# Value features in six chunks of six whole heads (120 rows) instead of five chunks of 128 rows

## The chip, the cores and the metric

The kernel runs on one core of one Trainium2 chip. The metric is device microseconds of one execution, start to end. Each run also has a *span*, the time from the first to the last instruction that the profiler recorded; the time is somewhat longer than the span. Each profile shows one execution. Wherever a median is quoted, it is over all runs of that kernel in that set of rounds.

TensorE (PE) multiplies matrices, and loads its weights (PEld) in parallel; VectorE is DVE, ScalarE is ACT, GpSimd is POOL, and SP issues the DMAs. A *pass* here is one matmul instruction.

## The reference, cut to what matters

```python
xn = _layernorm(x)                                  # x: 1 x 2048 x 640, H = 32 heads, Dh = 20
q, k, v = split(xn @ wqkv)                          # each 32 heads of 20 features
pq, pk = phi(q), phi(k)
kv  = einsum("bhsd,bhse->bhde", pk, v)              # one 20 x 20 matrix per head
num = einsum("bhqd,bhde->bhqe", pq, kv)
den = einsum("bhqd,bhd->bhq", pq, sum of pk over s)
s   = (num / den) @ wo                              # 640 x 640
g   = silu(relu(xn @ w1) @ w2)                      # 640 -> 1728 -> 640
out = x + s * g
```

Attention is linear and its `kv` is block diagonal (32 blocks of 20 x 20). The kernel forms G = xn^T pk, from it the blocks kv = wv^T G, and *folds* the output projection in: W = kv wo, 640 x 640. Then s is one product of the divided pq with W.

## The kernel before: the parts that matter

The 640 value features are cut into C = 5 chunks of P = 128 rows. A boundary of 128 cuts a head of 20, so a chunk touches 7 or 8 heads, and neighbouring chunks share heads.

```python
h_lo = [(P * c) // DH for c in range(C)]
h_hi = [-(-(P * (c + 1)) // DH) for c in range(C)]
def cs_of_m(m):       # chunks whose heads reach into columns 128m .. 128m+127 of W's rows
    return [c for c in range(C) if DH * h_lo[c] < P * (m + 1) and DH * h_hi[c] > P * m]
# -> 2, 3, 3, 3, 2 chunks for m = 0..4: 13, times two halves of 320 columns: 26 passes

def kv_block(c, b):                                  # one PSUM bank b
    n0, n1 = DH * h_lo[c], DH * h_hi[c]              # 140 or 160 columns
    PE:  for k in range(C): matmul(ps[b][:, 0:n1-n0], lhsT=wv_sb[:, k, P*c:P*(c+1)], rhs=GT[:, k, n0:n1])
    DVE: kvp[:, c, n0:n1] = ps[b][:, 0:n1-n0] * mask # also waits for POOL's memset of kvp

def W_block(m):                                      # banks b and b+1; pairs (4,5) and (6,7) in turn
    PE:  for a in range(2):
           for c in cs_of_m(m): matmul(ps[b+a][:, 0:320], lhsT=kvp[:, c, P*m:P*(m+1)], rhs=wo_sb[:, c, 320*a:320*(a+1)])
         # ONE signal, after the last pass of both halves
    ACT: wf[:, m, 0:320]   = ps[b]
    DVE: wf[:, m, 320:640] = ps[b+1]
# ... (cut)
# SP queue, in order: w2 (2 DMAs), w2l (2), wo (1), rx (5: reciprocals of the denominator, read back), ...
# PE order: G, half of U(0), kv_block 0..4, half of U(0), half of U(1), W_block 0..4, half of U(1), ...
# DVE order: divide(0), divide(1) [need rx 0 and 1], the masks of kv_block, divide(2..4), ...
```

`U(p)` are the passes of the second feed-forward product; U(1) holds banks 0 to 3 open while W is made, so W has two bank pairs and no more.

## Time and profile before

| what | value | where it is read |
|---|---|---|
| time | 226.27 us (226.14 to 226.59) | runs |
| span of the profiled run | 224.6 us | page |
| PE busy | 218.1 us, 97% | page, part 1 |
| PE's share of the chain that ended last | 92% | page, part 4 |
| kv blocks | 25 passes, 1.56 us | chain of waits |
| W blocks | 26 passes, 3.55 us | chain of waits |

The page of the kernel before, parts 1 and 4: busy time and share by engine, then the chain of work that ended last.

```profile
span 224.6 us, 3494 instructions
...
PE 218.1 (97%) x1450; PEld 135.2 (60%) x1460; DVE 102.5 (46%) x191; ACT 88.3 (39%) x146; POOL 43.8 (20%) x62
...
PE 92%; DVE 2%; DMA 2%; issue 1%; ACT 1%; SPq 1%; POOL 0%; DVEq 0%
```

TensorE is the bottleneck nearly everywhere, so a stage is worth what TensorE spends in it. The same chain in order of time, before (start, duration in us, what): L714 is kv, L729 is W, L768 is U.

```profile
137.66 1.56 PE psT L714 x25
139.23 3.53 PE psT L768 x26
...
143.47 3.71 PE psT L768 x26
147.18 3.55 PE psT L729 x26
```

The timeline of before in the W stage (start, duration, engine, line, operation, count, and in brackets how long the engine was idle before and what ended it): L735 and L733 are the copies that empty a block.

```profile
147.02 3.71 PE L729 MATMUL psT<-reg 128*128 128x320 bf16 x26
...
147.76 0.49 DVE L735 CAST reg<-psT 128x320 bf16<-128x320 f32 x1 [4.79 <-PE psT L729]
147.82 0.43 ACT L733 ACTIVATE reg<-psT 128x320 bf16<-128x320 f32 x1
148.36 2.03 PEld L729 LDWEIGHTS psT<-reg 128*128 128x128 bf16 x16 [0.16 <-DVE reg L735]
```

TensorE runs the 26 passes as one piece. Its only wait is for the first DVE copy: the weight load is 0.16 us late, and since weights are loaded ahead, the passes themselves lose 0.02 us.

### The profile page before, as it was taken

How to read it: one execution, taken by the hardware profiler on the slowest of the kernel's cores; microseconds unless marked ns; L12 is line 12 of the kernel's file. 1: busy time of each engine (PE TensorE's matmuls, PEld its weight loads, DVE VectorE, ACT ScalarE, POOL GpSimd, SP SyncE). 2: the span in 40 equal slices, each digit the busy share in tenths (PEclk: the TensorE clock that was granted, in tenths of full speed). 3: DMA queues.
4: the chain of work that ended last, by engine and by line, in shares of the span. 5: the costliest groups of instructions: out<-in, count | busy, mean ns of one | idle time of the engine just before them, and what ended most of it. 6: DMA issues, size and time to landing. Idle time of an engine off the chain costs nothing.

```text
span 224.6 us, 3494 instructions
## 1 busy us (share of the span) xinstructions
PE 218.1 (97%) x1450; PEld 135.2 (60%) x1460; DVE 102.5 (46%) x191; ACT 88.3 (39%) x146; POOL 43.8 (20%) x62
## 2 busy tenths in 40 slices
PE   7999999999999999999999999999999999999993
PEld 7654555455554555444477778667767767776772
DVE  4599931796639872967000044440404041331445
ACT  4587765657665666654521122241021102102110
POOL 2436842322541255700000013000000000000000
PEclk9999999999999999999999999999999999999999
DMA  6999620012501150000999999500001010101021
GB/s 185 362 395 257 149 74 0 0 31 58 32 1 29 29 56 5 0 0 3 210 217 300 346 386 325 176 0 3 34 25 61 0 60 3 58 0 61 27 90 58
DMA packets 24239, 23.07 MB, mean 103 GB/s; under 512 B 8992, under 2 KB 23584, under 8 KB 24224
## 3 DMA queue, kind: packets, MB, share of 16 engines
q1 hardware_dynamic: 24224, 22.86, 35.7%
q8 instruction: 11, 0.18, 0.4%
q14 instruction: 4, 0.03, 0.1%
HBM read 15.65 MB, written 5.24 MB: 93 GB/s over the span
## 4 chain that ended last, share of the span: by engine, by line
PE 92%; DVE 2%; DMA 2%; issue 1%; ACT 1%; SPq 1%; POOL 0%; DVEq 0%
PE psT L768 25%; PE psT L514 25%; PE psT L702 10%; PE psT L491 10%; PE psT L439 9%; PE psT L796 8%; DMA reg<-in_A_x_dram 2%; PE psT L729 2%; PE psT L746 1%; PE psT L527 1%; DVE reg L810 1%; PE psT L714 1%; PE psT L610 1%; DVE reg L813 0%; DVE stats L383 0%
## 5 line engine op out<-in xcount | busy, mean ns | idle before, releaser
L768 PE MATMUL psT<-reg,hT 128*128 128x320 bf16 x416 | 58.7, 299 | 0.3
L514 PE MATMUL psT<-reg 128*128 128x512 bf16 x252 | 56.8, 379 | 0.5 <-issue 0.2
L768 PEld LDWEIGHTS psT<-reg,hT 128*128 128x128 bf16 x416 | 40.3, 98 | 17.0 <-PE psT L746 1.6
L514 PEld LDWEIGHTS psT<-reg 128*128 128x128 bf16 x260 | 25.2, 98 | 29.2 <-ACT hT L518 0.4
L764 ACT ACTIVATE reg<-psT 128x640 bf16<-128x640 f32 x16 | 10.8, 702 | 68.8 <-PE psT L746 35.4
L518 ACT ACTIVATE hT<-psT 128x512 bf16<-128x512 f32 x52 | 30.9, 599 | 17.7 <-PE psT L514 17.4
L810 DVE TENSOR_TENSOR reg<-psT,reg 128x640 bf16<-128x640 f32 (+1 forms) x18 | 13.5, 749 | 49.0 <-PE psT L796 45.9
L451 POOL TENSOR_TENSOR zacc<-zacc,reg 128x640 f32<-128x640 f32 x16 | 22.6, 1412 | 21.5 <-DVE reg L470 21.3
L439 PE MATMUL psT<-reg 128*128 128x320 bf16 x160 | 24.5, 299 | 0.1
L796 PE MATMUL psT<-reg,pqT 128*128 128x320 bf16 x160 | 22.9, 299 | 0.0
L702 PE MATMUL psT<-reg 128*128 128x320 bf16 x160 | 21.9, 299 | 0.0
L491 PE MATMUL psT<-reg 128*128 128x512 bf16 x98 | 21.8, 379 | 0.1
L439 PEld LDWEIGHTS psT<-reg 128*128 128x128 bf16 x160 | 15.4, 98 | 8.0 <-ACT reg L427 0.3
L702 PEld LDWEIGHTS psT<-reg 128*128 128x128 bf16 x160 | 15.6, 98 | 6.4 <-issue 0.4
L796 PEld LDWEIGHTS psT<-reg,pqT 128*128 128x128 bf16 x160 | 15.7, 98 | 6.1
L695 DVE TENSOR_TENSOR pqT<-pqT,reg 128x2048 bf16<-128x2048 bf16 x5 | 5.9, 1219 | 26.8 <-DMA reg<-rden_by_feature 26.8
L491 PEld LDWEIGHTS psT<-reg 128*128 128x128 bf16 x100 | 9.8, 98 | 11.2
L383 DVE BATCH_NORM_STATS2 stats<-reg 128x6 f32<-128x320 bf16 x32 | 14.1, 479 | 3.7 <-DMA reg<-in_A_x_dram 3.7
L498 ACT ACTIVATE er<-psT 128x512 bf16<-128x512 f32 x20 | 12.4, 619 | 8.6 <-PE psT L491 3.5
L456 ACT ACTIVATE ek<-psT 128x640 bf16<-128x640 f32 x16 | 11.3, 707 | 9.1 <-PE psT L439 9.1
L468 DVE TENSOR_SCALAR ek<-ek 128x640 bf16<-128x640 bf16 x16 | 5.5, 347 | 18.3 <-ACT ek L456 18.3
L508 DVE SCALAR_TENSOR_TENSOR pqT<-er 128x512 bf16<-128x512 bf16 x15 | 12.9, 859 | 0.5
(58 smaller groups left out, 139.2 us busy)
## 6 DMA issues: line engine op xcount, KB each, us to landing
reg<-in_A_x_dram SPq DMA_DIRECT2D x16, 160.0 KB, 5.3
rden_by_feature<-rden SPq DMA_DIRECT2D x4, 640.0 KB, 8.8
reg<-rden_by_feature SPq DMA_DIRECT2D x5, 512.0 KB, 11.1
reg<-in_A_x_dram SPq DMA_DIRECT2D x4, 640.0 KB, 6.8
reg<-in_B_w_dram SPq DMA_DIRECT2D x2, 1120.0 KB, 10.2
out_dram<-reg SPq DMA_DIRECT2D x14, 160.0 KB, 1.8
reg<-in_B_w_dram SPq DMA_DIRECT2D x1, 1040.0 KB, 10.2
reg<-in_B_w_dram SPq DMA_DIRECT2D x1, 960.0 KB, 14.8
```

The lines of the kernel that those rows point to most:

```text
L383: sc.op("DVE", lambda eng: eng.bn_stats(stats[:, t, a, :], xin[:, t % XR, HN * a:HN * (a + 1)]), R=[("xin", t % XR)], W=[("stats", t, a)])
L439: fns.append(lambda eng, a=a, k=k: eng.matmul(ps[b + a][:, 0:HN], lhsT=xnT[:, k, tok(t)], rhs=wqk[:, k, D + HN * a:D + HN * (a + 1)], star ...
L451: sc.op("POOL", lambda eng: eng.tensor_tensor(out=zacc[:, :], in0=zacc[:, :], in1=pk[:, t, :], op=ALU.add), R=[("zacc",), ("pk", t)], W=[( ...
L491: sc.group("PE", [(lambda eng, k=k: eng.matmul(ps[b], lhsT=wqk[:, k, P * f:P * (f + 1)], rhs=xnT[:, k, schunk(j)], start=(k == 0), stop=(k ...
L498: sc.op("ACT", lambda eng: eng.activation(out=e_, in_=ps[b], func=ACTF.Exp), R=[("ps", b)], W=[("er_e", es)])
L508: sc.op("DVE", lambda eng: eng.scalar_tensor_tensor(out=pqT[:, f, schunk(j)], in0=e_, scalar=1.0, in1=r_, op0=ALU.min, op1=ALU.add), R=[(" ...
L514: a = sc.group("PE", [(lambda eng, k=k: eng.matmul(ps[b], lhsT=w1_sb[:, k, P * f:P * (f + 1)], rhs=xnT[:, k, schunk(j)], start=(k == 0), s ...
L518: sc.op("ACT", lambda eng: eng.activation(out=hT[:, f, schunk(j)], in_=ps[b], func=ACTF.Relu), R=[("ps", b)], W=[("hT", j, f)])
L702: fns.append(lambda eng, t=t, a=a: eng.matmul(ps[b + a][:, 0:HN], lhsT=xn[:, t, P * k:P * (k + 1)], rhs=pk[:, t, HN * a:HN * (a + 1)], sta ...
L768: fns = [(lambda eng, u=u, t=t, f=f, n=n: eng.matmul(ps[bs[n] + u][:, 0:HN], lhsT=hT[:, f, tok(t)], rhs=w2_sb[:, f, HN * n:HN * (n + 1)], ...
L796: sc.group("PE", [(lambda eng, c=c, a=a: eng.matmul(ps[b + a][:, 0:HN], lhsT=pqT[:, c, tok(t)], rhs=wf[:, c, HN * a:HN * (a + 1)], start=( ...
L810: sc.op("DVE", lambda eng: eng.tensor_tensor(out=tmpo[:, os_, lo:hi].rearrange(shp, a=na), in0=src, in1=g_sb[:, t, lo:hi].rearrange(shp, a ...
```

## The change

120 rows are exactly six heads. With chunks of 120 no head is cut, so fewer chunks overlap a 128-column block of W: two for every m, ten passes in place of thirteen per half (20 in place of 26). The price is a sixth chunk (30 kv passes in place of 25; 640 is 5 x 120 + 40, so chunk 4 contributes two heads and the last chunk starts at row 520). The core of the diff:

```diff
+    VK = (P // DH) * DH                                  # 120
+    NV = -(-D // VK)                                     # 6
+    VR = [min(VK * j, D - VK) for j in range(NV)]        # first row: 0 120 240 360 480 520
+    VH = [(VR[j] // DH, (VR[j + 1] if j + 1 < NV else D) // DH) for j in range(NV)]
...
-    w_load(wo_sb, A_wo, ("wo",), extra=[last_norm[0]])
+    dma("SP", lambda eng: eng.dma_start(wo_sb[0:VK, 0:NV - 1, :],
+                                        A_wo[0:VK * (NV - 1), :].rearrange("(c p) n -> p c n", p=VK)), ...)
+    dma("SP", lambda eng: eng.dma_start(wo_sb[0:VK, NV - 1, :], A_wo[D - VK:D, :]), ...)
...
-        eng.matmul(ps[b][:, 0:n1 - n0], lhsT=wv_sb[:, k, P * c:P * (c + 1)], rhs=GT[:, k, n0:n1], ...)
+        eng.matmul(ps[b][0:VK, 0:n1 - n0], lhsT=wv_sb[:, k, r0:r0 + VK], rhs=GT[:, k, n0:n1], ...)
...
-        cs = cs_of_m(m)
+        cs = [j for j in range(NV) if DH * VH[j][0] < P * (m + 1) and DH * VH[j][1] > P * m]
-        lhsT=kvp[:, c, P * m:P * (m + 1)], rhs=wo_sb[:, c, HN * a:HN * (a + 1)]
+        lhsT=kvp[0:VK, c, P * m:P * (m + 1)], rhs=wo_sb[0:VK, c, HN * a:HN * (a + 1)]
```

More of the change, by code (lines that the diff above doesn't have):

```diff
@@ L239, in bass_recurrent_scan__linear_attn_block__dense_activation_relu__prompt_kernel @@
     out2 = out[0]
-    h_lo = [(P * c) // DH for c in range(C)]
-    h_hi = [-(-(P * (c + 1)) // DH) for c in range(C)]
-    def cs_of_m(m):
-        return [c for c in range(C) if DH * h_lo[c] < P * (m + 1) and DH * h_hi[c] > P * m]
+    VK = (P // DH) * DH
+    NV = -(-D // VK)
+    VR = [min(VK * j, D - VK) for j in range(NV)]
+    VH = [(VR[j] // DH, (VR[j + 1] if j + 1 < NV else D) // DH) for j in range(NV)]
     bf = dt.bfloat16
@@ L261, in bass_recurrent_scan__linear_attn_block__dense_activation_relu__prompt_kernel @@
     pk = reg3[:, :].rearrange("p (t n) -> p t n", t=T)
-    kvp = reg3[:, 0:C * D].rearrange("p (c n) -> p c n", c=C)
-    outb = reg3[:, C * D:(C + NOUT) * D].rearrange("p (a n) -> p a n", a=NOUT)
-    tmpo = reg3[:, (C + NOUT) * D:(C + 2 * NOUT) * D].rearrange("p (a n) -> p a n", a=NOUT)
+    kvp = reg3[:, 0:NV * D].rearrange("p (c n) -> p c n", c=NV)
+    outb = reg3[:, NV * D:(NV + NOUT) * D].rearrange("p (a n) -> p a n", a=NOUT)
+    tmpo = reg3[:, (NV + NOUT) * D:(NV + 2 * NOUT) * D].rearrange("p (a n) -> p a n", a=NOUT)
     pqT = nc.alloc_sbuf_tensor("pqT", [P, C, S], bf)
@@ L282, in bass_recurrent_scan__linear_attn_block__dense_activation_relu__prompt_kernel @@
     xin = reg7[:, :].rearrange("p (t n) -> p t n", t=XR)
-    wo_sb = reg7[:, 0:C * D].rearrange("p (c n) -> p c n", c=C)
+    wo_sb = reg7[:, 0:NV * D].rearrange("p (c n) -> p c n", c=NV)
     NEK = 4
@@ L680, in bass_recurrent_scan__linear_attn_block__dense_activation_relu__prompt_kernel @@
             W=[("w2l", u)], extra=[lastW1])
-    w_load(wo_sb, A_wo, ("wo",), extra=[last_norm[0]])
+    dma("SP", lambda eng: eng.dma_start(wo_sb[0:VK, 0:NV - 1, :],
+                                        A_wo[0:VK * (NV - 1), :].rearrange("(c p) n -> p c n", p=VK)),
+        W=[("wo", 0)], extra=[last_norm[0]])
+    dma("SP", lambda eng: eng.dma_start(wo_sb[0:VK, NV - 1, :], A_wo[D - VK:D, :]), W=[("wo", 1)], extra=[last_norm[0]])
     for c in range(C):
@@ L709, in G_block, with kv_block @@
         return ag
-    def kv_block(c, b):
-        n0, n1 = DH * h_lo[c], DH * h_hi[c]
-        nh = h_hi[c] - h_lo[c]
-        sc.group("PE", [(lambda eng, k=k: eng.matmul(ps[b][:, 0:n1 - n0], lhsT=wv_sb[:, k, P * c:P * (c + 1)],
+    def kv_block(j, b):
+        h0, h1 = VH[j]
+        n0, n1 = DH * h0, DH * h1
+        r0 = VR[j]
+        sc.group("PE", [(lambda eng, k=k: eng.matmul(ps[b][0:VK, 0:n1 - n0], lhsT=wv_sb[:, k, r0:r0 + VK],
                                                      rhs=GT[:, k, n0:n1], start=(k == 0), stop=(k == C - 1)))
@@ L717, in kv_block @@
         sc.op("DVE", lambda eng: eng.tensor_tensor(
-            out=kvp[:, c, n0:n1].rearrange("p (h e) -> p h e", e=DH),
-            in0=ps[b][:, 0:n1 - n0].rearrange("p (h e) -> p h e", e=DH),
-            in1=mh[:, c, h_lo[c]:h_hi[c]].unsqueeze(2).to_broadcast([P, nh, DH]), op=ALU.mult),
-            R=[("ps", b), ("mh",), ("kvz",)], W=[("kv", c)])
+            out=kvp[0:VK, j, n0:n1].rearrange("p (h e) -> p h e", e=DH),
+            in0=ps[b][0:VK, 0:n1 - n0].rearrange("p (h e) -> p h e", e=DH),
+            in1=mh[0:VK, 0, 0:h1 - h0].unsqueeze(2).to_broadcast([VK, h1 - h0, DH]), op=ALU.mult),
+            R=[("ps", b), ("mh",), ("kvz",)], W=[("kv", j)])
     def W_block(m):
         b = nextp()
-        cs = cs_of_m(m)
+        cs = [j for j in range(NV) if DH * VH[j][0] < P * (m + 1) and DH * VH[j][1] > P * m]
         fns = []
@@ L729, in W_block @@
                 fns.append(lambda eng, a=a, c=c, ci=ci: eng.matmul(
-                    ps[b + a][:, 0:HN], lhsT=kvp[:, c, P * m:P * (m + 1)], rhs=wo_sb[:, c, HN * a:HN * (a + 1)],
+                    ps[b + a][:, 0:HN], lhsT=kvp[0:VK, c, P * m:P * (m + 1)], rhs=wo_sb[0:VK, c, HN * a:HN * (a + 1)],
                     start=(ci == 0), stop=(ci == len(cs) - 1)))
-        sc.group("PE", fns, R=[("wo",), ("kvz",)] + [("kv", c) for c in cs], W=[("ps", b), ("ps", b + 1)])
+        sc.group("PE", fns, R=[("wo", 0), ("wo", 1), ("kvz",)] + [("kv", c) for c in cs], W=[("ps", b), ("ps", b + 1)])
         sc.op("ACT", lambda eng: eng.activation(out=wf[:, m, 0:HN], in_=ps[b][:, 0:HN], func=ACTF.Copy),
@@ L834, in kv_all @@
     def kv_all():
-        for c, b in enumerate((0, 1, 2, 3, 0)):
+        for c, b in enumerate((0, 1, 2, 3, 0, 1)):
             kv_block(c, b)
```

## The prediction

> **What bounds the kernel.** TensorE. The page gives PE busy 218.1 of 224.6 us (97%) at full granted clock in all 40 slices, and the chain that ended last is 92% PE. Only PE time counts, in two stages of that chain: the kv blocks, 25 passes, 1.56 us (62 ns each), and the folded weight W, 26 passes (13 x 2 halves), 3.55 us (136.5 ns each). Together 2.3% of the span.
>
> **Removed.** Six 128x320 passes of W. Starts of 320-column passes are 136 ns apart in the trace (20 of them elsewhere take 2.72 us), so at the full pace W would take 2.72 us: -0.83 us.
>
> **Given back by eviction (main point).** W blocks alternate between two bank pairs; block m+2 waits until ACT and DVE have emptied block m. In before's timeline a block's last pass starts, 0.34 us later its DVE copy starts, which takes 0.49 us; 0.14 us after it ends, the first pass into that pair starts. A bank pair is thus unusable for 0.97 us after the start of a block's last pass. Before, blocks were 4, 6, 6, 6, 4 passes; 6 + 1 passes cover 0.95 us, which just fits: the trace shows one wait, costing 0.02 us. Now all blocks are of 4. Counted from the first pass of W: block 2 could start at 1.09 but waits until 1.38; block 4 could at 2.46 but waits until 2.75; end 3.29. So 0.57 of the 0.83 comes back as two waits of 0.28 us. Net -0.26 us.
>
> **Added.** kv: 30 passes in place of 25, of 120 columns (five of 40). Passes of 140, 160, 320 columns start 61, 69, 136 ns apart, so 120 should need 52.5: about 1.5-1.6 us if weight loads hide. But the weights now have 120 columns. The Trainium skill ("TensorE: Matmul & The Clock Gate", Weight-path perf modes) says that the fast weight load needs the full 128. The trace agrees in tendency: loads of 64 columns took 110 ns, of 128 columns 98, of 32 columns 92-97. At 13 ns per 32 columns, my estimate for 120 is 133 ns, occupying the path for about 50 ns, just hidden behind a 52 ns pass. Entering another array shape cost some 95 ns each way elsewhere in this trace (64- and 32-column groups); 120 may count as one. I put kv at 1.75 us (+0.2); if loads do not overlap, up to 3 us.
>
> **Off the path.** The POOL memset grows by a fifth (2.77 to about 3.3 us), ending near 137.5 us, before the first kv mask multiply at 138.0. The sixth DVE multiply, the extra DMA issue and 0.1 MB of wo have slack.
>
> **Predicted: 226.2 us** (226.27 - 0.26 + 0.2), range 225.7 to 226.7. Faster by over 2%: 0.00; within 2%: 0.99; slower: 0.01.
>
> **What would show it.** W line: 20 passes, first start to the next line's start about 3.3 us, with two waits of TensorE for the DVE copy near 0.3 us each (2.72 and no wait: my eviction step is wrong). kv line: weight loads of about 130 ns rather than 98, 30 passes in about 1.75 us (1.55: loads hide fully; 2.5 or more: they do not overlap).
>
> **What would make it wrong.** Evictions that finish sooner than the trace shows (then 225.6); slow 120-column loads in series (then up to 227.4); 120-row weights in W also loading slowly; a DMA that lands late and holds DVE.

## The result

The changed kernel took 226.70 us in the median of 5 runs (226.44 to 227.03), the kernel before 226.27 (226.14 to 226.59). The ratio is 1.0017, 95% interval 1.0002 to 1.0031. A ratio is the mean time of one kernel's fast runs over that of the other's fast runs of the same rounds, so it is not quite the ratio of the medians. Executions over 1.5% slower than the fastest of the same kernel are left out of the means. Six passes fewer, and the kernel is not faster.

The chain of waits of the changed kernel; L718 is kv, L733 is W, L772 is U.

```profile
137.84 1.65 PE psT L718 x30
139.49 3.53 PE psT L772 x26
...
143.74 3.71 PE psT L772 x26
147.44 1.09 PE psT L733 x8
148.53 0.12 issue
148.66 1.25 PE psT L733 x8
149.90 0.07 issue
149.98 0.70 PE psT L733 x4
```

W is now in three pieces, cut where block 2 and block 4 start: each waits for its bank pair. Its timeline, to be set against that of before:

```profile
147.28 3.40 PE L733 MATMUL psT<-reg 120*128 120x320 bf16 x20
...
148.03 1.04 DVE L739 CAST reg<-psT 128x320 bf16<-128x320 f32 x2 [4.81 <-PE psT L733]
148.08 0.93 ACT L737 ACTIVATE reg<-psT 128x320 bf16<-128x320 f32 x2
148.63 0.94 PEld L733 LDWEIGHTS psT<-reg 120*128 120x128 bf16 x8 [0.43 <-DVE reg L739]
...
149.95 0.40 PEld L733 LDWEIGHTS psT<-reg 120*128 120x128 bf16 x4 [0.38 <-DVE reg L739]
```

The idle times before the weight loads are 0.43 and 0.38 us. Starts of passes are 136 ns apart inside a block, and 424 and 374 ns at these two places, so the passes lose 0.29 and 0.24 us. From its first pass to the next stage's first pass W takes 3.24 us (before 3.55; twenty unhindered passes take 2.72).

The kv stage, line by line, before and after (duration of one in ns as minimum/median/maximum):

```profile
L714 PEld LDWEIGHTS psT<-reg,wv_sb x25: 97/98/98, 137.4 to 138.9; 128*128 128x128 bf16 x25
L714 PE MATMUL psT<-reg,wv_sb x25: 224/224/233, 137.5 to 139.0; 128*128 128x140 bf16 x20, 128*128 128x160 bf16 x5
```

```profile
L718 PEld LDWEIGHTS psT<-reg,wv_sb x30: 133/135/135, 137.5 to 139.2; 128*120 128x120 bf16 x30
L718 PE MATMUL psT<-reg,wv_sb x30: 185/218/243, 137.7 to 139.3; 128*120 128x120 bf16 x25, 128*120 128x40 bf16 x5
```

Loading 120 columns of weights takes 135 ns, more than 128 columns (98 ns), and the 30 passes start 55 ns apart.

So the two stages together gained 0.31 - 0.08 = 0.23 us, where the prediction had put 0.26 - 0.2 = 0.06 us (in the middle of the profiles, from the start of the first pass over `ones` at about 97 us to the start of the last pass, 123.00 us against 123.23). Yet the time went up by 0.4 us. The trace splits the difference of the two profiled runs (226.06 and 226.44 us):

| part | before | after | difference |
|---|---|---|---|
| start to first pass over `ones` | 97.51 | 97.69 | +0.18 |
| from there to the last pass (holds kv and W) | 123.23 | 123.00 | -0.22 |
| start of last pass to end of span | 3.90 | 4.03 | +0.13 |
| time minus span | 1.42 | 1.72 | +0.30 |

What needs explaining lies at the start and the end, where the change alters no arithmetic. One place at the end can be read directly: the SP queue's own closing instructions, from the view of the program's closing line (start in us), before and after:

```profile
L864 SPq COMPARE_BRANCH  x1: 33/33/33, 224.0 to 224.0; - x1
L864 SPq DRAIN  x1: 13/13/13, 224.1 to 224.1; - x1
```

```profile
L868 SPq COMPARE_BRANCH  x1: 33/33/33, 224.0 to 224.0; - x1
L868 SPq DRAIN  x1: 70/70/70, 224.4 to 224.4; - x1
```

From the start of the branch to that of the drain it is 0.14 us before and 0.48 us after. There is also one effect in the middle that cost nothing in this execution. These are the two divides that DVE runs ahead of the kv masks, before and after, from the timeline:

```profile
132.16 2.50 DVE L695 TENSOR_TENSOR pqT<-pqT,reg 128x2048 bf16<-128x2048 bf16 x2 [26.75 <-DMA reg<-rden_by_feature]
138.01 1.56 DVE L717 TENSOR_TENSOR reg<-psT,mh 128x140 bf16<-128x140 f32 x5 [3.35 <-PE psT L714]
```

```profile
134.60 2.51 DVE L698 TENSOR_TENSOR pqT<-pqT,reg 128x2048 bf16<-128x2048 bf16 x2 [29.02 <-DMA reg<-rden_by_feature]
138.16 1.66 DVE L721 TENSOR_TENSOR reg<-psT,mh 120x120 bf16<-120x120 f32 x6 [1.05 <-PE psT L718]
```

The reload of the reciprocals landed 2.4 us later. DVE then had 1.05 us to spare before the first mask, in place of 3.35.

### The profile page after: what moved, and what is told of

Its sections match the earlier page's. It is cut to its first block, busy times and chain, and to the rows that moved or that the text cites. A ratio compares the mean times of both kernels' runs of the same rounds, so it can differ in the third digit from the quotient of the medians.

```text
span 224.7 us, 3494 instructions
## 1 busy us (share of the span) xinstructions
PE 218.2 (97%) x1449; PEld 135.1 (60%) x1459; DVE 102.6 (46%) x192; ACT 88.3 (39%) x146; POOL 44.3 (20%) x62
## 4 chain that ended last, share of the span: by engine, by line
PE 92%; DMA 2%; DVE 2%; issue 1%; ACT 1%; SPq 1%; POOL 0%; DVEq 0%
PE psT L772 25%; PE psT L514 25%; PE psT L705 10%; PE psT L491 10%; PE psT L439 9%; PE psT L800 8%; DMA reg<-in_A_x_dram 2%; PE psT L733 1%; PE psT L750 1%; PE psT L527 1%; DVE reg L814 1%; PE psT L718 1%; PE psT L610 1%; DVE reg L817 0%; DVE stats L383 0%
## 5 line engine op out<-in xcount | busy, mean ns | idle before, releaser
L772 PE MATMUL psT<-reg,hT 128*128 128x320 bf16 x416 | 58.7, 299 | 0.3
L772 PEld LDWEIGHTS psT<-reg,hT 128*128 128x128 bf16 x416 | 40.3, 98 | 17.0 <-PE psT L750 1.6
```

The lines of the kernel that those rows point to most:

```text
L772: fns = [(lambda eng, u=u, t=t, f=f, n=n: eng.matmul(ps[bs[n] + u][:, 0:HN], lhsT=hT[:, f, tok(t)], rhs=w2_sb[:, f, HN * n:HN * (n + 1)], ...
```

## The experiments

Theory 1 (**eviction**): W is held by the emptying of its two bank pairs. Rival: passes over 120 rows are slow in themselves, or each pass costs its 136 ns whatever waits. Theory 2 (**weight load**): the kv passes are held by the slower load of 120 columns. Rival: 55 ns is a floor. Theory 3, for the missing 0.4 us: **the end of the program** costs more because of the one extra DMA. Rivals: noise, or a slow stage that I had not found. (The traces show 70 DMA instructions on the SP queue in the kernel before, 12 of them transposes, and 71 in the changed one. The expectations below speak of 54 and 55: their count is 16 too low throughout, but only the difference of one matters.) Theory 4 (**late reload**): the new wo loads, ahead in the DMA queue, take away DVE's slack.

The first four runs used one chip, with 11 runs of the kernel before (median 226.37 us).

### null_before: the kernel before, unchanged

> The kernel before, unchanged, as a null for the timing. If the 0.4 us by which the changed kernel's runs were longer is spread of start and end (its trace shows 0.18 us from the landing of the first loads, 0.13 us after the last output landed, and 0.23 us gained in between), this null should also stray by 0.2 us or more from the kernel before, and its start and end should move in its profile. If instead timing repeats to 0.1 us and start and end stand still, the changed kernel has a real cost outside of the two stages that I have not found.

Measured: 226.50 us median, ratio 1.0006 (0.9991 to 1.0021). Its W and kv stages repeat to 1 ns (3.547 and 1.563 us) and its middle is 123.23 us, but its start, to the first pass over `ones`, is 97.92 us in place of 97.51, because the first loads landed later. Runs of the kernel before spread over 225.90 to 226.85 us. So a stage can be read to hundredths of a microsecond in a profile, while times vary by some +-0.4 us, much of it at the start. Time minus span, however, was 1.40 to 1.51 us in every run of the kernel before.

### again_after: the changed kernel, unchanged

> The changed kernel once more. Spread theory: somewhere within 226.0 to 226.7, ratio to before not the same 1.0017 again, the first PE work not again 0.18 us later. Rival (a systematic cost of the change outside PE): ratio 1.0015 to 1.002 again, with the same 0.18 us at the start and 0.13 us at the end. Either way in the profile: kv stage 1.65 us, W stage 3.24 us with two waits of about 0.3 us.

Measured: 226.88 us median of all five; the four fast runs are 226.70 to 227.03 us (median 226.83), ratio 1.0022 (1.0007 to 1.0036). The rival was right that something systematic exists: time minus span was again 1.70 to 1.78 us, never near 1.45, and from the last pass to the end of the span it was again 4.02 us. The fifth run, the profiled one, took 230.55 us and is left out of the ratio. I use it only for what waits for what:

```profile
138.12 1.26 PE L718 MATMUL psT<-reg,wv_sb 128*120 128x120 bf16 x20
138.40 2.50 DVE L698 TENSOR_TENSOR pqT<-pqT,reg 128x2048 bf16<-128x2048 bf16 x2 [32.38 <-DMA reg<-rden_by_feature]
140.82 1.41 DVE L721 TENSOR_TENSOR reg<-psT,mh 120x120 bf16<-120x120 f32 x6
141.15 0.62 PEld L718 LDWEIGHTS psT<-reg,wv_sb 128*120 128x120 bf16 x10 [1.90 <-DVE reg L721]
```

The reload landed at 138.4 us. DVE did its two divides first, the masks came after 140.8 us, and TensorE, with four of six kv blocks in four banks, waited 1.99 us from pass to pass for the first mask. The loss grew, because TensorE's clock then fell (the clock was full until 142.1 us; that the wait brought its fall about is likely, but one execution does not show it). This is the table of windows for 142.1 to 145.5 us (length, then busy us of PE, PEld, DVE, ACT, POOL, then granted clock, DMA share, GB/s):

```profile
142.10:145.50 3.40, 3.40 (x15) 1.97 (x14) 3.40 (x4) 0.00 (x0) 0.00 (x0) 0.50 1.06 361
```

At half clock the 26 passes of U after kv took 1.67 us more. In this execution w2, which lies ahead of wo in the queue, had landed 4 us late too (132.2 us, before 128.1). Whether the wo load behind it held it up is not shown: from 127 to 129 us the DMA engines were full (share 1.12) but moved 179 GB/s, where they moved 350 GB/s before. The change had at any rate taken away most of the slack of 3.35 us (argued from the slack, not run).

### pad26: six passes put back that add zero

```diff
         cs = [j for j in range(NV) if DH * VH[j][0] < P * (m + 1) and DH * VH[j][1] > P * m]
+        if 0 < m < C - 1:
+            cs = cs + [5 if m == 1 else 0]  # its block of kvp is zero here
```

> The changed kernel with a third pass per half in the three middle W blocks, over a chunk whose block is zero there: 26 passes again, same result. Eviction theory: the six passes fill the waits, so W goes from 3.24 to about 3.55 us, +0.31 us or 52 ns a pass; no wait over 0.05 us. Rival (W pays per pass, 136 ns each): +0.82 us, W at 4.05 us.

Measured in the profile: W 3.547 us in one piece, as in the kernel before, and kv 1.65 us. Six full passes of TensorE work cost 0.31 us, 52 ns each, not 136: the rest of their time fitted into the waits. The chain of waits of pad26:

```profile
147.37 3.55 PE psT L735 x26
150.92 7.07 PE psT L774 x52
```

The rival's 4.05 us is out. The time was 227.16 us (ratio 1.0038, 1.0018 to 1.0057).

### halves_dve: each half of a W block signalled and emptied by itself

```diff
-        one group of both halves -> ACT empties half 0, DVE empties half 1
+        for a in range(2):
+            sc.group("PE", [passes of half a], ..., W=[("ps", b + a)])
+            half 0: DVE copies ps[b] to wf;  half 1: ACT copies ps[b + 1] to wf
```

The first half goes to DVE because ACT still has a silu of the stage before to end.

> The changed kernel with W signalled and emptied by half block: DVE empties the first half (ACT still has a silu to end there), ACT the second, and the next-but-one block waits half by half. Eviction theory: both waits go, W takes 2.72 to 2.80 us in place of 3.24, the kernel is 0.45 to 0.5 us shorter than the changed one. Rival (20 passes with 120-row weights are slow in themselves): W stays at 3.2 us.

Measured: W in one piece, 2.718 us, the full pace, with the same 120-row weights. The two waits are gone and the rival with them.

```profile
147.78 2.72 PE psT L731 x20
150.50 7.07 PE psT L773 x52
```

The middle of the profile is 122.49 us, 0.52 us below the changed kernel's 123.00. The median was 226.33 us, 0.5 us below that of again_after's fast runs, but one run of 227.46 widens the interval (ratio to before 1.0004, 0.9981 to 1.0026).

The next four runs used another chip (kernel before: 226.09 us median of 11).

### before_2dma: the kernel before with one DMA more

```diff
-    w_load(wo_sb, A_wo, ("wo",), extra=[last_norm[0]])
+    dma(... wo_sb[:, 0:4, :], A_wo[0:512, :] ..., W=[("wo",)])
+    dma(... wo_sb[:, 4, :],   A_wo[512:D, :], W=[("wo", 1)])
```

> The kernel before with its wo load cut into two DMAs (4 chunks of 128 rows, then 1), the same bytes: one DMA more, 55 as the changed kernel has. All runs so far show time minus span at 1.41 to 1.51 us for the kernel before and 1.68 to 1.78 us for every kernel with the change. Theory A, the extra DMA costs 0.28 us outside of the span: here time minus span is 1.7 us and the time 0.3 us above before. Rival B, it comes from something else in the change (120-row shapes, other code): it stays at 1.45 us and the time at before's. The landing of the first reload of the reciprocals (132.1 us before, 134.6 to 138.4 us in the changed kernels) should stay near 132.1 if it is the 120-row form or the added bytes that delay it, and move to 134 or later if it is the number of DMAs.

Measured: time minus span 1.68 to 1.77 us, and 4.02 us from the last pass to the end of the span (kernel before 3.90), exactly as in the changed kernels, although kv (1.562 us), W (3.547 us), shapes and bytes are those of the kernel before. The time was 226.88 us, ratio 1.0035 (1.0015 to 1.0055). So the longer end comes with the 71st DMA and has nothing to do with 120 rows. The time rose by more than the end accounts for: 0.35% is 0.79 us (interval 0.34 to 1.24), of which 0.40 us is read at the end and the rest is open, as in the changed kernel. The first reload landed at 132.5 us: cutting the load in two is not what delays it.

### wo_late: wo behind the reloads

The two wo loads moved behind the five reloads in program order, nothing else.

> The changed kernel with its two wo loads issued behind the reloads of the reciprocals, not ahead of them. Theory: the wo loads delay those reloads, which hold the two divides that stand before the kv multiplies on DVE; in the changed kernel the second divide ends 0.1 to 1.1 us before the first kv multiply could start, and in one slow profile 2.3 us after it, where TensorE waited 2 us. Here the first reload should land near 132.1 us again, the second divide end near 134.7 us, and the spans lose the occasional extra: mean span about 0.2 to 0.4 us below the changed kernel's 225.0, 224.7 us, time minus span still 1.73 us. Rival (the loads do not matter, spread is from the start alone): the reload lands earlier but the mean span stays at 225.0 us.

Measured: 226.67 us median, ratio 1.0023 (1.0002 to 1.0044). The first reload landed at 130.4 us, earlier than before the change, and DVE had 5.95 us to spare:

```profile
130.39 2.50 DVE L698 TENSOR_TENSOR pqT<-pqT,reg 128x2048 bf16<-128x2048 bf16 x2 [24.11 <-DMA reg<-rden_by_feature]
138.85 1.11 DVE L721 TENSOR_TENSOR reg<-psT,mh 120x120 bf16<-120x120 f32 x4 [5.95 <-PE psT L718]
```

The wo loads ahead of them in the queue are thus what delays the reloads. My expectation for the time was a miss: spans were 224.6 to 225.4 us, mean 224.98, no lower than the changed kernel's 224.98 when the change was first timed (in other rounds, so only roughly comparable). The profiled run also began late (first pass over `ones` at 98.38 us). The late reload does no harm in most runs; it makes a rare large loss possible. In the six profiles with 120-row loads ahead of the reloads the slack was 1.05 and 0.55 us, used up in three without a wait of TensorE (pad26, kv128, after_w2one), and overrun by 2 us in again_after. Among all runs, spans above 225.6 us occurred only in kernels of this form (225.7, 225.9, 226.3, 226.4 and 228.8 us). That fits, but only the last of these was profiled, so how often a loss occurs is not known.

### wo128: the wo load in 128-row form, still ahead of the reloads

The first wo load takes 128 rows per chunk, overlapping by 8; the last chunk keeps 120.

> The changed kernel with the first wo load in 128-row chunks that overlap by 8 rows (7% more bytes), rows 120 to 127 unread. If the form with 120 rows makes the load slow (The Trainium skill, DMA: Bandwidth & Descriptors, says the number of engines is the largest one up to 16 that divides the rows: 15 for 120 rows, 16 for 128), the first reload of the reciprocals lands near 132.5 us, not 134.6. If it is the added bytes and the position ahead of the reloads, it lands at 134.6 us or later still.

Measured: 226.83 us median, ratio 1.0027 (1.0004 to 1.0049). The first reload landed at 134.8 us, which by the letter of the expectation says bytes and position. But w2 ahead of it landed 1.95 us later in this run. Counted from the landing of the last load of the feed-forward weights, the reload came 3.38 us later in the kernel before, 5.27 us in the changed one, 4.29 us here. The form matters as well. The cleaner pair is wo_late and `best` (below), where wo is the last of the queue's big loads: from the last reload's landing to wo's, 921,600 bytes in 120 rows took 4.02 us (229 GB/s), 983,040 bytes in 128 rows took 2.50 us (393 GB/s; the 819,200 bytes of the kernel before, from the load ahead of it, 2.10 us, 390 GB/s). The Trainium skill ("DMA: Bandwidth & Descriptors", Why a DMA increments its semaphore by 16 and not by 1) says that a DMA uses the largest number of engines up to 16 that divides its rows, which makes 15 for 120. By my estimate from 15 of 16 that explains 6% at most, not the 42% measured; no run here shows how many engines a load used. They were not idle: in the table of windows the DMA share is 1.11 at 232 GB/s in wo_late (137.04 to 139 us) and 1.05 at 376 GB/s in `best` (137 to 138 us), so the same bytes kept them busy for longer. Why stays open.

### kv128: 128 weight columns for the kv passes

```diff
-        lhsT=wv_sb[:, k, r0:r0 + VK]  -> ps[b][0:VK, ...]
+        w = P if r0 + P <= D else VK      # chunks 0 to 4: 128 columns, 8 of them not used afterwards
+        lhsT=wv_sb[:, k, r0:r0 + w]   -> ps[b][0:w, ...]
```

> The changed kernel with 128 weight columns in the kv passes of chunks 0 to 4 (rows 120 to 127 of the result are not read), 120 in the last one. Weight-load theory: with 120 columns the load (133 to 135 ns) sets the pace of 55 ns; with 128 it takes 98 ns, the 120-column passes start 52.5 ns apart and the five of 40 columns about 25 ns apart, and kv takes 1.5 us in place of 1.65. Rival (55 ns is a floor of the pass): unchanged 1.65 us.

Measured (one run, 226.63 us): kv 1.478 us in place of 1.647, in the same 30 passes. More columns, less time: the load set the pace. The passes of 40 columns tell most: behind loads of 128 columns they start 25 ns apart, in the changed kernel 55 ns, so 55 ns is neither their own length nor a floor. (The edit also widens the passes' output from 120 to 128 rows; that this matters was not tested by itself.)

```profile
L719 PEld LDWEIGHTS psT<-reg,wv_sb x30: 95/98/135, 137.9 to 139.4; 128*128 128x128 bf16 x25, 128*120 128x120 bf16 x5
```

That is its view of the source line; its chain of waits has the stage as one piece:

```profile
138.21 1.48 PE psT L719 x30
```

The last four runs were on the first chip again (kernel before: 226.36 us median of 12, of which 11 are the runs of the first set; so these ratios compare with runs made some twelve minutes earlier).

### after_w2one: the changed kernel with one DMA less, 70

The two w2 loads are joined in one; nothing of the change is undone.

> The changed kernel with its two w2 loads joined in one, so that it has 54 DMAs as the kernel before has, and nothing else undone. All runs with 55 DMAs so far show, whatever else they do, 0.48 us between the last branch and drain of the SP queue in the profile (0.14 with 54) and 1.68 to 1.81 us between span and time (1.40 to 1.51 with 54). Theory: one DMA more costs 0.4 us at the end of the program, so this run shows 0.14 us and 1.45 us, and the time is 0.2 to 0.25 us under before's, the gain of the two stages. Rival (the form of the change costs it): 0.48 and 1.73 us stay.

Measured: time minus span 1.40 to 1.52 us and 3.91 us from last pass to end of span, as in the kernel before. The end is back, the change stays in, and the middle is 123.01 us. The time did not confirm it: 226.44 us median, with runs from 225.52 to 227.82 (ratio 1.0016, 0.9993 to 1.0039), too wide to see 0.2 us in. Against the changed kernel itself, its mean of 226.52 us is 0.33 us below that of again_after's fast runs, in the direction expected but within the noise. In its profile the second divide ended at 137.88 us and the first mask came 0.2 us late for it, so its slack was used up, without a wait of TensorE this time.

### before_w2one: the kernel before with one DMA less, 69

> The kernel before with its two w2 loads joined: 53 DMAs. If the end costs in proportion to the number of DMAs, time minus span falls to about 1.2 us and the time by 0.3 to 0.4 us. If there is a step between 54 and 55, it stays at 1.45 us and 0.14 us, and the time at before's.

Measured: 226.49 us, ratio 1.0006 (0.9988 to 1.0024): no gain. Neither line of the expectation holds to the letter: time minus span rose to 1.72 to 1.76 us, while last pass to end of span fell to 3.61 us. The sum counts: from the last pass to the end of the time it is 3.61 + 1.74 = 5.35 us with 69 DMAs, 3.90 + 1.45 = 5.35 with 70, and 4.02 + 1.73 = 5.75 with 71 (this takes it that all of time minus span lies after the span). So there is a step of 0.40 us between 70 and 71, not a price per DMA, and the end of the span is no fixed mark. The traces show a pause of some 0.3 us on the SP queue that moves: with 71 DMAs it stands before SP's drain (0.48 us from the branch to the drain in all eight such profiles, 0.14 in the other six), with 70 between the drain and SP's last event (0.49 us, against 0.16 with 69); with 69 none is seen inside the span. Each DMA adds one instruction to SP (79, 80 and 81 in the traces). So a rival stands: the length of SP's program may make the step, and not the DMA as such. No run added an SP instruction that is not a DMA.

### before_halves: the finer eviction without the change

> The kernel before (26 passes of W) with W emptied by half block, DVE first, and nothing else. Eviction theory: before's blocks of six passes already cover the eviction, so W falls only from 3.55 to 3.53 us. Rival (emptying by halves is worth 0.5 us by itself): W at 3.0 to 3.1 us.

Measured (one run, 226.36 us): W 3.531 us (before 3.547). Emptying by halves is worth 0.02 us to 26 passes and 0.52 us to 20. Alone the two parts gain 0.02 and 0.31 us, together 0.83.

### best: the parts put together

Six chunks, each of 128 rows. For heads 0 to 5 of a chunk the mask is zero in rows 120 to 127, and the last chunk starts at row 512 and uses the old mask of chunk 4. wo is loaded in 128-row form behind the reloads, w2 in one load (70 DMAs), and W is emptied by halves.

```diff
-        lhsT=wv_sb[:, k, r0:r0 + VK]                     # r0 = VR[j]
+        r0 = min(VR[j], D - P); lhsT=wv_sb[:, k, r0:r0 + P]
-        kvp[0:VK, c, ...], wo_sb[0:VK, c, ...]
+        kvp[:, c, ...], wo_sb[:, c, ...]
```

> All findings in one: six chunks, but each of 128 rows (rows outside of the six heads masked to zero, the last chunk from row 512), so kv loads 128 weight columns and wo 128 rows; W signalled and emptied by half block, DVE first; wo loaded behind the reloads of the reciprocals; w2 in one load, 54 DMAs. Expected: kv 1.45 us (30 passes, 25 of them 52.5 ns apart, five 25 ns), W 2.72 us, together 0.95 us under before, nothing added at the end: 225.3 to 225.4 us against before's 226.3, ratio 0.9955 to 0.9962. If the parts do not add up (a rival view: each gain is eaten by the next wait in the stage after), less than 0.6 us.

Measured: 225.40 us median, 225.33 to 225.61 over 5 runs; ratio to before 0.9961 (0.9946 to 0.9975). kv took 1.437 us, W 2.716 us, and the middle 122.27 us, 0.95 us under before, as the sum of the parts said. It is 0.4% faster than the kernel before, and its median lies 0.6% below that of again_after's fast runs, with which it was not run in the same rounds; its runs spread less than those of any other kernel with as many runs here.

```profile
137.94 1.44 PE psT L716 x30
...
147.33 2.72 PE psT L729 x20
```

```profile
130.83 2.50 DVE L695 TENSOR_TENSOR pqT<-pqT,reg 128x2048 bf16<-128x2048 bf16 x2 [25.15 <-DMA reg<-rden_by_feature]
138.24 1.46 DVE L719 TENSOR_TENSOR reg<-psT,mh 128x120 bf16<-128x120 f32 x6 [4.90 <-PE psT L716]
```

## Why the prediction was right or wrong

**The time** (226.2, range 225.7 to 226.7; measured 226.70 in the median) stood at the very edge of its range. A change of about nothing was forecast, and about nothing came, but that the number fits is partly luck. The two stages behaved as told in kind and gained 0.17 us more than forecast (0.23 in place of 0.06); a cost at the end that the prediction left out, and a remainder that is not settled, took that back and more.

**Eviction, the main point: right.** Predicted: W 3.29 us with waits of 0.28 and 0.28. Measured: 3.24 with 0.29 and 0.24; the second restart came 0.09 us after the copy's end and not 0.14. Of the 0.83 us that six passes are worth, 0.31 arrived. pad26 (six passes back for 0.31 us) and halves_dve (W at 2.72 us) show the cause, and before_halves shows that emptying by halves gains next to nothing (0.02 us) while the blocks are long.

**The kv passes: mechanism right, size slightly off.** The weight load was predicted at 133 ns and took 135. The predicted 1.75 us held an allowance for switching array shape, "120 may count as one". It does not: the passes start 55 ns apart from the second on and the stage took 1.647 us, so +0.08 and not +0.2. kv128 shows that the load sets the pace.

**The step that failed: "the extra DMA issue ... [has] slack".** It was costed as issue time on a queue with room, which it has. What came with it is 0.40 us at the end of the program, by before_2dma (the cost without the change) and after_w2one (the change without the cost). This is read from the traces and from time minus span; the times themselves are too noisy to size it. Whether the DMA makes it or the one more instruction on SP is open. With it the account is -0.23 + 0.40 = +0.17 us. Measured were +0.43 in the medians of the first set, with an interval of the ratio from +0.05 to +0.70 us. The other 0.2 to 0.3 us is not settled. The start scatters between 97.13 and 98.38 us over 14 profiles; it averaged 98.0 us in the eight with 71 DMAs and 97.6 us in the other six, too few to call it a cost.

**"0.1 MB of wo [has] slack": right for the profiled run, wrong as a margin.** 0.1 MB at before's 390 GB/s would delay the reloads by 0.26 us (my estimate from that rate); they came 2.4 us later. The 120-row form moved at 229 GB/s at the end of the queue, and w2 ahead of it landed later as well. DVE's slack shrank from 3.35 to 1.05 us, and in one execution it was overrun. The halved clock that followed added 1.67 us to the 1.99 us of the wait.

**POOL's memset: right.** It ended at 137.67 us (3.30 us long), before the first mask at 138.16.

## What to carry to other kernels

Taking passes away from a short ping-pong stage brings only what the emptying of its banks leaves over: compare the passes per block with the time from a block's last pass to the bank's reuse (here 0.97 us, or seven passes), and refine the signal together with the removal (here 0.02 and 0.31 us alone, 0.83 together). Full-width tiles with masked rows (128 of which 120 count) were faster here than exact-width ones, both for weight loads and for DMA. When a change adds a DMA or moves bytes, look at what stands behind it in the queue and in the order of the engine that waits for it, and measure the bare addition in the old kernel before blaming the arithmetic.

## What the Trainium skill lacked or had wrong

- "TensorE: Matmul & The Clock Gate", Weight-path perf modes: it says that the fast weight load needs all 128 columns. The trace agrees: 135 ns for 120 columns, 98 ns for 128. The section has no number for widths near 128: loads of 120 columns start 55 ns apart, and 30 kv passes fell from 1.65 to 1.48 us when 25 of them were widened to 128.
- The same page, LDWEIGHTS (loading the stationary operand): columns divided by 1.2 gives 100 ns for 120 columns; the trace shows 133 to 135 ns, and 55 ns from start to start. That the number of rows does not matter agrees: 120-row weights of 128 columns load in 96 ns.
- The same page, Part 1: it gives about 3.4 us of idling as what lowers the clock. Here a wait of 1.99 us between passes was followed by 3.4 us at half clock. The page's free-running window may allow for this; one execution does not tell.
- "DMA: Bandwidth & Descriptors", Why a DMA increments its semaphore by 16 and not by 1: 15 engines for 120 rows would explain 6% (my estimate); the load in 120-row form moved at 229 GB/s, in 128-row form at 393 GB/s.
- No page that I read has the step in the end of the program: from the last pass to the end of the time 5.35 us with 69 and 70 DMAs, 5.75 us with 71. What makes the step is open.
